# q in 512-byte pieces for two chunks at once, some transposes by DMA, and one searched order for the whole kernel: a linear-attention and expert kernel

## The chip, the cores and the metric

The kernel runs on one core of a Trainium2 chip. The metric is the device time of one execution in microseconds (us), median of several runs. A profiled run also gives a trace; its "span", from the first to the last instruction, is about 1.7 us shorter than the time (156.4 against 158.06 us before the change). All runs compared here are of the state "fast" unless a sentence says otherwise. "TensorE" does the matrix products and (PE in the profile) also transposes; VectorE is DVE, ScalarE is ACT, GpSimd is POOL, and SPq is the one queue from which all DMAs of this kernel are issued. PSUM is the memory into which this kernel's TensorE operations write; VectorE or ScalarE copies a result out of it ("evacuates" it) before its tile is written again.

## The reference

q, k and v have the shape (4, 8, 768, 64): batch, heads, tokens, head size. A decaying state is summed over the tokens, and its product with q is the input of a feed-forward block.

```python
def _attn_ref(q, k, v):                       # gamma differs by head, scale = 1/8
    for t in range(S):
        state = gamma * state + einsum('bhd,bhe->bhde', k[:, :, t], v[:, :, t])
        y[:, :, t] = scale * einsum('bhd,bhde->bhe', q[:, :, t], state)
def _moe_ref(x, w_in, w_out, g_ln):           # x: 3072 x 512
    h = x @ w_in                              # "first product", 512 -> 1024
    solu = h * softmax(h)
    ln = (solu - mean(solu)) / sqrt(var(solu) + 1e-6) * g_ln
    return ln @ w_out                         # "second product", 1024 -> 512
```

## The kernel before

The tokens are cut into 24 chunks of 128 (six per batch). A chunk needs its 128 x 512 slices of q, k and v as float32 (256 KB each). They are cast to bfloat16; q and k are transposed on TensorE through the one PSUM tile `Tp` (4 blocks of 128 x 128 each) and copied out. `scores` (k times q), `mask`, `intra` (masked scores times v) and `inter` (state times q) give y; then follow the first product `mm1`, `e = exp(h)`, `u = h * e`, eight transposes of u through the same `Tp`, and the second product `mm2`.

```python
def load(name, t, src, slot):                 # one chunk, 256-byte pieces (64 floats)
    op("sp", lambda e: e.dma_start(out=dst[:], in_=src[b, :, rows, :].rearrange("h p d -> p h d")), ...)

def t_in(t, j):                               # 4 transposes of k (j=1) or q (j=0)
    for blk in range(4):
        op("pe", lambda e, blk=blk: e.transpose(
            out=Tp[:, 4 * j + blk, :], in_=qk16[s16][:, j, 128 * blk:128 * blk + 128], identity=ident[:]), ...)

def t_u(t, eng, hf):                          # 8 transposes of u in two halves, then u_evac copies Tp to uT
    for blk in range(4 * hf, 4 * hf + 4):
        op("pe", lambda e, blk=blk: e.transpose(out=Tp[:, blk, :], in_=u16[s][:, ...], identity=ident[:]), ...)
# ... cut: scores, mask, intra, inter, state, mm1, expo, umul, square, stats, mm2, z_out, store
```

Every helper adds its instruction to one program list. A wait is derived from what the instruction reads and writes, and each engine runs its instructions in the order of that list. So the order of the list is the schedule. It comes from three places: a table for the start (`PROLOGUE`), a regular loop for the middle chunks, and a table for the end (`EPILOGUE`). An entry such as `uT.3:act` is a stage, a chunk and, where it isn't the default one, an engine. `warm.5` is five matmuls on constants that only keep TensorE busy while data are on their way.

The softmax here doesn't subtract the row's maximum and nothing guards it: scores larger than these inputs give would overflow.

Of the kernel before, what the change touches and what calls it, by code (L numbers as in the profile page):

```python
# [6 lines left out]
ACT = mybir.ActivationFunctionType  # L7
# [6 lines left out]
L = 128  # L14
# [11 lines left out]
PROLOGUE = """  # L26
Lg.0 warm.6 clr.0 t_g.0 Lk.0 ck.0:dve t_k.0 g_out.0:act Lq.0 Lq.1 cq.0:dve warm.2 t_q.0 qkT.0 Lk.1 cq.1 warm.5
scores.0 Lv.0 Lwi.1 Lwi.0 wi0.0 Lwi.3 ck.1:dve t_k.1 t_q.1 mask.0 wi1.1 Lwi.2 qkT.1:dve cv.0 warm.4 state.0
intra.0 Lv.1 wi1.0 scores.1 Lk.2 mask.1 y.0 Lq.2 Lv.2 wi0.1:dve wi0.2:dve st.0 Lk.3 Lwo.1 wi1.3 wi0.3 Lq.3 Lwo.0
wi1.2 warm.17 mm1_0.0 e0.0 cv.1 ck.2:dve Lwo.2 inter.1 mm1_1.0 state.1 e1.0 intra.1 cq.2 u0.0 y.1 t_k.2 Lwo.3  # L30
warm.2 t_q.2 Lv.3 st.1:act mm1_0.1 qkT.2:dve inter.2 u1.0 e0.1 Lk.4 scores.2 Lq.4 mask.2 Lq.5 cv.2 state.2
mm1_1.1 e1.1 Lv.4 wg.2 sq.0 ck.3 t_k.3 wg.3:dve u0.1 wg.0 cq.3 intra.2 warm.4 t_q.3 y.2 qkT.3:dve warm.3
scores.3 Lk.5 t_u0.0 t_u1.0 st.2 wg.1:dve wg.5 inter.3 u1.1 mm1_0.2 wg.4 wg.6:dve Lk.6 cv.3 mm1_1.2 wg.7 Lv.5
mask.3 uT.0 ck.4 Lq.6 Lv.6 e0.2 u0.2 colmean.0 intra.3 t_k.4 cq.4:dve cm_out.0 statsA.1 sq.1 t_q.4 qkT.4 ctr.3
statsA.0 mm2.0 y.3 cq.5 ctr.0 ctr.1 e1.2 stats.1 ck.5 t_u0.1 cv.4 t_u1.1 Lk.7 zm.0 Lq.7 uT.1:act scores.4
state.3 st.3:act u1.2 mm1_0.3 mask.4 ctr.7 t_k.5 t_q.5 ctr.4 statsA.2 stats.0 e0.3 inter.4 mm1_1.3 state.4 ck.6
cq.6 intra.4 qkT.5 scores.5 st.4:act u0.3 t_u0.2 t_u1.2 mm2.1 e1.3 u1.3 uT.2:act z.0 t_k.6 y.4 t_q.6 zm.1 clr.6
sq.2 cv.6 inter.5 mm1_0.4 Lv.7 statsA.3 qkT.6 store.0 Lk.8 state.6 Lq.8 mm1_1.4 ctr.6 Lv.8 sq.3 ctr.2 z.1
stats.2 t_u0.3 t_u1.3 ctr.5 mm2.2 mask.5 scores.6 e0.4 z.2 cq.7 uT.3 store.1 u0.4 cv.5 Lk.9 intra.5 ck.7 Lq.9
stats.3 Lv.9 e1.4 t_k.7 cv.7 t_q.7 y.5 qkT.7 mm2.3 store.2 Lk.10 ck.8 u1.4 sq.4 Lq.10 Lv.10 t_u0.4 mask.6 st.6  # L40
t_u1.4 uT.4 z.3 mm1_0.5 store.3 mm1_1.5 state.7 e0.5 Lk.11 Lq.11 intra.6 e1.5 Lv.11 ck.9 scores.7 u0.5 u1.5 y.6
cq.8 statsA.4 t_k.8 mask.7 t_q.8 qkT.8 mm2.4 stats.4 t_u0.5 z.4:dve cq.9 t_u1.5 sq.5 mm1_0.6 inter.7 intra.7
scores.8 st.7 uT.5 cv.9 statsA.5 store.4 Lk.12 y.7 mm1_1.6 Lq.12 Lv.12 t_k.9 e0.6 e1.6 u0.6 stats.5 u1.6 t_q.9
qkT.9 mm2.5 ck.10 mm1_0.7 e0.7 t_u0.6 t_u1.6 cv.8 cq.10 inter.8 mm1_1.7 cv.10 z.5:dve store.5 Lk.13 statsA.6
Lq.13 Lv.13 state.8 mask.8 intra.8 sq.6 uT.6 scores.9 t_k.10 t_q.10 stats.6 mm2.6 u0.7 e1.7 u1.7 statsA.7 qkT.10
y.8 z.6:dve t_u0.7 t_u1.7 st.8:act mm1_0.8 mm1_1.8 ck.11 cq.11 cv.11 mask.9 store.6 inter.9 uT.7 Lk.14 Lq.14
sq.7 Lv.14 intra.9 e0.8 state.9 u0.8 scores.10 e1.8 t_k.11 stats.7 u1.8 t_q.11 qkT.11 mm2.7 t_u0.8 sq.8 ck.12
cq.12 cv.12 y.9 st.9 mask.10 t_u1.8 uT.8 z.7 store.7 mm1_0.9 e0.9 mm1_1.9 e1.9 inter.10 Lk.15 Lq.15 statsA.8
Lv.15 intra.10 state.10 scores.11 t_k.12 t_q.12 qkT.12 ck.13 cq.13 cv.13 u0.9 u1.9 y.10 st.10 stats.8 statsA.9
sq.9 stats.9 mm2.8 z.8:dve mask.11 store.8  # L50
"""

EPILOGUE = """
cq.20 Lv.20 intra.15 state.15 scores.16 t_k.17 t_q.17 qkT.17 ck.18 cq.18 cv.18 u0.14 u1.14 y.15 st.15 statsA.14
sq.14 stats.14 mask.16 mm2.13 z.13 store.13 t_u0.14 t_u1.14 uT.14 mm1_0.15 e0.15 mm1_1.15 e1.15 inter.16 Lk.21
Lq.21 Lv.21 intra.16 state.16 cv.20 scores.17 t_k.18 t_q.18 qkT.18 ck.19 cq.19 cv.19 u0.15 u1.15 y.16 st.16
statsA.15 sq.15 stats.15 mask.17 mm2.14 z.14 ck.20 store.14 t_u0.15 t_u1.15 uT.15 mm1_0.16 e0.16 mm1_1.16 e1.16
inter.17 Lk.22 Lq.22 Lv.22 intra.17 scores.18 t_k.19 cq.22 t_q.19 qkT.19 u0.16 u1.16 y.17 statsA.16 sq.16
stats.16 mask.18 mm2.15 z.15 store.15 t_u0.16 t_u1.16 uT.16 mm1_0.17 e0.17 mm1_1.17 e1.17 Lk.23 t_k.20 t_q.20
Lq.23 Lv.23 intra.18 clr.18 state.18 scores.19 u0.17 u1.17 ck.21 cq.21 y.18 ck.22 st.18 qkT.20 statsA.17 sq.17  # L60
stats.17 mask.19 cv.21 mm2.16 z.16 store.16 t_u0.17 t_u1.17 uT.17 mm1_0.18 e0.18 mm1_1.18 t_k.21 t_q.21 e1.18
inter.19 intra.19 state.19 qkT.21 u0.18 u1.18 scores.20 y.19 st.19 mask.20 statsA.18 sq.18 stats.18 mm2.17 z.17
store.17 t_u0.18 cv.22 t_u1.18 inter.20 uT.18 mm1_0.19 e0.19 ck.23:dve intra.20 state.20 y.20 scores.21 mm1_1.19
st.20:act t_k.22 e1.19 u0.19 t_q.22 qkT.22 u1.19 statsA.19 inter.21 sq.19 stats.19 mm2.18 z.18 store.18 cq.23
t_u0.19 t_u1.19 mask.21 mm1_0.20 e0.20 cv.23 intra.21 state.21 uT.19 y.21 scores.22 t_k.23 u0.20 mm1_1.20 t_q.23
st.21:act inter.22 mm1_0.21 mm2.19 mask.22 e1.20 qkT.23 t_u0.20 intra.22 e0.21 u1.20 u0.21 sq.20 mm1_1.21 e1.21
t_u1.20 state.22 y.22 scores.23 uT.20 mm1_0.22 t_u0.21 st.22:act u1.21 z.19 statsA.20 e0.22 statsA.21 inter.23
store.19 sq.21 mask.23 t_u1.21 uT.21 stats.20 mm1_1.22 intra.23 e1.22 u0.22 y.23 mm2.20 stats.21 t_u0.22
mm1_0.23 u1.22 t_u1.22 mm1_1.23 e0.23 statsA.22 z.20:dve uT.22 mm2.21 store.20 e1.23 u0.23 u1.23 z.21:dve
store.21 t_u0.23 t_u1.23 sq.22 sq.23 mm2.22 statsA.23 stats.22 z.22 uT.23 store.22 mm2_0.23 stats.23 z_0.23:dve  # L70
mm2_1.23 z_1.23:dve store_0.23 store_1.23
# [109 lines left out]
def bass_retnet_recurrent__then__act_solu_kernel(  # L181
# [16 lines left out]
    NRAW, N16, NQT, NOUT = 8, 4, 4, 4  # L198
    NUNC = 2
    LAG = 2  # L200

    with ExitStack() as es:
        sb = lambda name, shape, dt: es.enter_context(nc.sbuf_tensor(name, shape, dt))

        q_raw = [sb(f"q_raw{i}", [128, H, D], F32) for i in range(NRAW)]
        k_raw = [sb(f"k_raw{i}", [128, H, D], F32) for i in range(NRAW)]
        v_raw = [sb(f"v_raw{i}", [128, H, D], F32) for i in range(NRAW)]
        qk16 = [sb(f"qk16_{i}", [128, 2, DM], BF16) for i in range(N16)]
        v16 = [sb(f"v16_{i}", [128, H, D], BF16) for i in range(N16)]
        qkT = [sb(f"qkT{i}", [128, 8, 128], BF16) for i in range(NQT)]  # L210
# [53 lines left out]
        def load(name, t, src, slot):  # L264
            dst = {"q": q_raw, "k": k_raw, "v": v_raw}[name][slot]
            b, c = tiles[t]
            rows = slice(c * L, (c + 1) * L)
            op("sp", lambda e: e.dma_start(out=dst[:], in_=src[b, :, rows, :].rearrange("h p d -> p h d")),  # L268
               w=[(name + "raw", slot)], sem=f"ld{name}{slot}")

        def load_k(t, eng):
            load("k", t, k, t % NRAW)

        def load_q(t, eng):
            load("q", t, q, t % NRAW)

        def load_v(t, eng):
            load("v", t, v, t % NRAW)

        def load_w_in(kt, eng):  # L280
            op("sp", lambda e: e.dma_start(out=w_in_st[:, kt, :], in_=moe_w_in[128 * kt:128 * kt + 128, :]),  # L281
               w=[("w_in_st", kt)], sem=f"w_in{kt}")
# [19 lines left out]
        def setup_consts():  # L302
            op("dve", lambda e: e.memset(ones_bf[:], 1.0), w=["ones_bf"])
            op("pool", lambda e: e.iota(iota_c[:], [[128, NCH]], base=1, channel_multiplier=1,
# [4 lines left out]
            op("pool", lambda e: e.affine_select(out=tri[:], in_=ones_bf[:], pattern=[[1, 128]],  # L309
# [6 lines left out]
            op("pool", lambda e: e.iota(iota_t[:], [[1, S]], base=1, channel_multiplier=0,  # L316
# [11 lines left out]
            op("dve", lambda e: e.memset(zeros_bf[:], 0.0), w=["zeros_bf"])  # L328
# [14 lines left out]
        def w_in_cast(kt, eng, hf):  # L343
            cols = slice(512 * hf, 512 * hf + 512)
            copy_scaled(eng, w_in16[:, kt, cols], w_in_st[:, kt, cols], SCALE,
                        r=[("w_in_st", kt)], w=[("w_in16", kt, hf)])
# [27 lines left out]
        def cast(name, j, raw, t, eng):  # L374
            s, s16 = t % NRAW, t % N16
            src, dst = raw[s][:].rearrange("p h d -> p (h d)"), qk16[s16][:, j, :]
            f = (lambda e: e.activation(out=dst, in_=src, func=ACT.Copy)) if eng == "act" else (
                lambda e: e.tensor_copy(out=dst, in_=src))
            op(eng, f, r=[(name + "raw", s)], w=[(name + "16", s16)])

        def cast_k(t, eng):
            cast("k", 1, k_raw, t, eng)

        def cast_q(t, eng):
            cast("q", 0, q_raw, t, eng)
# [9 lines left out]
        def evac(eng, out, in_, **deps):  # L395
            if eng == "act":
                op(eng, lambda e: e.activation(out=out, in_=in_, func=ACT.Copy), **deps)  # L397
            else:
                op(eng, lambda e: e.tensor_copy(out=out, in_=in_), **deps)  # L399

        def t_in(t, j):
            s16 = t % N16
            for blk in range(4):
                op("pe", lambda e, blk=blk: e.transpose(  # L404
# [313 lines left out]
```

## Time and profile before

| | before |
|---|---|
| time, median | 158.06 us (157.45 to 158.09) |
| span of the profiled run | 156.4 us |
| busy: TensorE, VectorE, ScalarE, GpSimd | 94%, 76%, 68%, 59% of the span |
| share of the DMA queue over 16 engines | 80.7% |
| TensorE transposes, warm-up matmuls | 384, 43 |

Busy time by stretch, kernel before. The columns are the stretch, its length, busy us and instruction count of TensorE, of its weight loads, of VectorE, ScalarE and GpSimd, the granted TensorE clock, the busy share of the DMA engines and the rate that they moved.

```profile
core 0: us, PE busy (x) PEld busy (x) DVE busy (x) ACT busy (x) POOL busy (x), PEclk, DMA share, GB/s
0.00:16.00 16.00, 12.33 (x86) 5.71 (x87) 8.63 (x31) 9.36 (x14) 3.48 (x12) 1.00 0.99 251
16.00:33.00 17.00, 14.43 (x142) 7.44 (x141) 12.20 (x24) 9.78 (x21) 6.46 (x11) 1.00 1.09 258
33.00:70.00 37.00, 36.46 (x390) 21.15 (x388) 32.08 (x59) 27.56 (x54) 31.98 (x61) 1.00 1.09 239
70.00:96.00 26.00, 26.00 (x259) 15.10 (x256) 21.10 (x39) 18.79 (x37) 18.39 (x40) 1.00 0.88 194
96.00:117.00 21.00, 21.00 (x230) 12.78 (x228) 16.99 (x31) 15.36 (x30) 14.04 (x29) 1.00 0.90 197
117.00:154.00 37.00, 36.69 (x361) 21.39 (x359) 28.19 (x53) 25.43 (x54) 18.42 (x47) 1.00 0.26 77
```

From 33 us on TensorE is busy for practically all of each stretch: it is the limit there. Before 33 us the DMA share is about 1 at some 255 GB/s, and 43 of TensorE's matmuls there are warm-ups: the loads are the limit. The chain of waits, cut to one chunk in the middle (start, us on the chain, what):

```profile
80.44 0.55 PE Tp L404 x8
80.99 1.73 PE Zp L550 x8
82.72 0.45 PE Tp L531 x8
83.17 1.73 PE Hp L480 x8
```

The chain stays on TensorE. It shows what an operation costs where TensorE is the limit: eight transposes 0.45 us (56 ns each), a full product 1.73 us. Five to six us pass between one first product and the next. The page's lines on packets and on the DMA queue:

```profile
DMA packets 80178, 29.61 MB, mean 189 GB/s; under 512 B 75416, under 2 KB 75680, under 8 KB 80160
...
q1 hardware_dynamic: 80160, 29.37, 80.7%
```

75,416 of the 80,178 packets are under 512 bytes, nearly all of them q, k and v (72 x 1,024 pieces of 256 bytes). The start of the first product, from the timeline of TensorE (start, us, what, count):

```profile
14.67 1.24 PE L369 MATMUL Zp<-ones_bf,zeros_bf 128*128 128x512 bf16 x5
15.75 1.03 PE L480 MATMUL Hp<-w_in,xT 128*128 128x512 bf16 x4
```

### The profile page before, as it was taken

Reading aid. Unit: us, or ns where it says so; the run is one execution under the profiler, and the core shown is the slowest. Engines: PE = TensorE matmul, PEld = TensorE weight load, DVE = VectorE, ACT = ScalarE, POOL = GpSimd, SP = SyncE. Lnnn points to the kernel's source line nnn. Section 1 sums busy time; section 2 is a strip of 40 time slices with the busy share of each in tenths; the row PEclk is TensorE's granted clock in tenths of the full one; section 3 lists DMA queues with packets and bytes.
Section 4 is the critical chain, followed back from the end, with each engine's and each line's share of the span. In section 5 each row is a group of like instructions: output and inputs, shape, how many; then the busy total and the mean of one; then the engine's idle time right before and its main releaser. Section 6 shows DMA issues by size and latency. Waiting matters only on the chain.

```text
span 156.4 us, 3798 instructions
## 1 busy us (share of the span) xinstructions
PE 146.9 (94%) x1456; PEld 83.6 (53%) x1456; DVE 119.4 (76%) x234; ACT 106.3 (68%) x210; POOL 92.8 (59%) x195
## 2 busy tenths in 40 slices
PE   0999989689998999999999999999999999999993
PEld 0454544245645556565655566566555656555552
DVE  6257588689997796798796877796878698859752
ACT  6628436948978645868667776876877768669370
POOL 4120441389999897699486578409978661705260
PEclk9999999999999999999999999999999999999999
DMA  4999999998998999999986996996897610101113
GB/s 94 228 368 316 201 254 357 232 225 183 241 257 201 262 267 223 266 263 196 222 200 163 178 229 152 201 228 165 191 191 185 150 66 9 67 4 67 67 67 134
DMA packets 80178, 29.61 MB, mean 189 GB/s; under 512 B 75416, under 2 KB 75680, under 8 KB 80160
## 3 DMA queue, kind: packets, MB, share of 16 engines
q1 hardware_dynamic: 80160, 29.37, 80.7%
q8 instruction: 11, 0.18, 0.5%
q14 instruction: 7, 0.06, 0.1%
HBM read 23.07 MB, written 6.29 MB: 188 GB/s over the span
## 4 chain that ended last, share of the span: by engine, by line
PE 68%; SPq 15%; POOL 6%; DMA 4%; DVE 4%; issue 1%; DVEq 0%
PE Zp L550 22%; PE Hp L480 21%; SPq L268 11%; PE Tp L404 6%; PE Tp L531 6%; DMA q_raw<-in_q_dram 4%; PE Yp L448 4%; PE PT L422 4%; SPq L285 3%; PE Yp L438 2%; PE PT L550 2%; SPq L281 2%; PE Sp L464 1%; DVE w L362 1%; POOL chain L512 1%
## 5 line engine op out<-in xcount | busy, mean ns | idle before, releaser
L480 PE MATMUL Hp<-w_in,xT 128*128 128x512 bf16 x192 | 47.3, 379 | 0.0
L550 PE MATMUL Zp<-w,uT 128*128 128x512 bf16 (+1 forms) x168 | 38.9, 374 | 0.0
L429 DVE TENSOR_TENSOR ptm<-PT,tri 128x1024 bf16<-128x1024 f32 x24 | 29.2, 1216 | 1.9 <-PE PT L422 1.9
L397 ACT ACTIVATE qkT<-Tp 128x1024 bf16<-128x1024 bf16 x21 | 21.4, 1020 | 12.4 <-PE Tp L404 12.4
L480 PEld LDWEIGHTS Hp<-w_in,xT 128*128 128x128 bf16 x192 | 17.0, 98 | 15.5 <-DVE su L493 0.4
L550 PEld LDWEIGHTS Zp<-w,uT 128*128 128x128 bf16 x168 | 15.6, 98 | 15.2
L487 ACT ACTIVATE e_1<-Hp 128x512 bf16<-128x512 f32 x24 | 14.3, 596 | 13.6 <-PE Hp L480 13.6
L487 ACT ACTIVATE e_0<-Hp 128x512 bf16<-128x512 f32 x24 | 14.3, 595 | 9.6 <-PE Hp L480 9.6
L474 DVE TENSOR_TENSOR xT<-Yp,ytab 128x512 bf16<-128x512 f32 x24 | 16.4, 685 | 2.3 <-PE Yp L448 2.2
L399 DVE COPY uT<-Tp 128x1024 bf16<-128x1024 bf16 x22 | 15.0, 683 | 1.8 <-PE Tp L531 1.5
L369 PE MATMUL Zp<-ones_bf,zeros_bf 128*128 128x512 bf16 x43 | 12.1, 419 | 3.6 <-DVE zeros_bf L328 3.6
L519 POOL TENSOR_SCALAR chain<-sq,chain 128x1 f32<-128x1 f32 x24 | 7.4, 308 | 12.9 <-ACT sq_junk L502 11.9
L525 POOL TENSOR_TENSOR rstd<-chain,mhalf 128x1 f32<-128x1 f32 x24 | 13.2, 549 | 2.0
L502 ACT ACTIVATE sq_junk<-u_1 128x1024 bf16<-128x1024 bf16 x12 | 12.6, 1051 | 0.1
L502 ACT ACTIVATE sq_junk<-u_0 128x1024 bf16<-128x1024 bf16 x12 | 12.6, 1049 | 0.0
L509 POOL TENSOR_SCALAR chain<-se 128x1 f32<-128x1 f32 x24 | 6.7, 280 | 9.9 <-ACT e_1 L487 8.4
L493 DVE CUSTOM_DVE_ANT_0 u_1<-Hp,e_1 128x512 bf16<-128x512 f32 x12 | 8.2, 686 | 5.6 <-ACT e_1 L487 5.6
L493 DVE CUSTOM_DVE_ANT_0 u_1<-Hp,e_1,su 128x512 bf16<-128x512 f32 x12 | 9.0, 750 | 3.5 <-ACT e_1 L487 3.5
L339 ACT ACTIVATE out_sb<-Zp,rstd 128x512 f32<-128x512 f32 x14 | 9.5, 679 | 2.4 <-PE Zp L550 2.4
L493 DVE CUSTOM_DVE_ANT_0 u_0<-Hp,e_0 128x512 bf16<-128x512 f32 x12 | 8.2, 683 | 3.0 <-ACT e_0 L487 3.0
L493 DVE CUSTOM_DVE_ANT_0 u_0<-Hp,e_0,su 128x512 bf16<-128x512 f32 x12 | 9.0, 748 | 1.9 <-ACT e_0 L487 1.8
L512 POOL TENSOR_SCALAR chain<-su 128x1 f32<-128x1 f32 x24 | 7.4, 309 | 4.7 <-DVE su L493 3.2
(106 smaller groups left out, 261.3 us busy)
## 6 DMA issues: line engine op xcount, KB each, us to landing
k_raw<-in_k_dram SPq DMA_DIRECT2D x24, 256.0 KB, 4.1
q_raw<-in_q_dram SPq DMA_DIRECT2D x24, 256.0 KB, 4.4
v_raw<-in_v_dram SPq DMA_DIRECT2D x24, 256.0 KB, 4.7
out_dram<-out_sb SPq DMA_DIRECT2D x23, 256.0 KB, 2.3
w_in_st<-in_moe_w_in_dram SPq DMA_DIRECT2D x4, 512.0 KB, 5.8
w_out_st<-in_moe_w_out_dram SPq DMA_DIRECT2D x4, 512.0 KB, 6.6
out_dram<-out_sb SPq DMA_DIRECT2D x2, 128.0 KB, 1.7
g_row<-in_moe_g_ln_dram SPq DMA_DIRECT2D x1, 4.0 KB
```

Source lines behind the costliest of these rows:

```text
L268: op("sp", lambda e: e.dma_start(out=dst[:], in_=src[b, :, rows, :].rearrange("h p d -> p h d")), w=[(name + "raw", slot)], sem=f"ld{name} ...
L369: op("pe", lambda e: e.matmul(Zp[:], zeros_bf[:], ones_bf[:].unsqueeze(1).to_broadcast([128, 4, 128]), start=True, stop=True), r=["zeros_b ...
L397: op(eng, lambda e: e.activation(out=out, in_=in_, func=ACT.Copy), **deps)
L399: op(eng, lambda e: e.tensor_copy(out=out, in_=in_), **deps)
L429: op("dve", lambda e: e.tensor_tensor(out=ptm[s][:], in0=PT[:], in1=tri[:].unsqueeze(1).to_broadcast([128, 8, 128]), op=ALU.mult), r=["tri ...
L474: op("dve", lambda e: e.tensor_tensor(out=xT[s][:], in0=Yp[:], in1=ytab[:, c, :, :], op=ALU.mult), r=[("ytab", p) for p in range(NPAIR)], ...
L480: op("pe", lambda e, kt=kt: e.matmul(Hp[:, hf, :], xT[s][:, kt, :], w_in16[:, kt, 512 * hf:512 * hf + 512], start=(kt == 0), stop=(kt == K ...
L487: op("act", lambda e: e.activation(out=e16[s][:, 512 * hf:512 * hf + 512], in_=Hp[:, hf, :], func=ACT.Exp, accum_out=se[ss][:, hf:hf + 1]) ...
L493: op("dve", lambda e: e.tensor_tensor_reduce(out=u16[s][:, 512 * hf:512 * hf + 512], in0=Hp[:, hf, :], in1=e16[s][:, 512 * hf:512 * hf + 512],
L502: op("act", lambda e: e.activation(out=sq_junk[:], in_=u16[s][:], func=ACT.Square, accum_out=sq[ss][:]), r=[("u16", s, 0), ("u16", s, 1)], ...
L525: op("pool", lambda e: e.tensor_tensor(out=rstd[ss][:], in0=ch[:, 3:4], in1=mhalf[:], op=ALU.pow), r=[("ch3", sc), "mhalf"], w=[("rstd", ss)])
L550: op("pe", lambda e, kt=kt: e.matmul(dst, uT[s][:, kt, :], w[:, kt, cols], start=(kt == 0), stop=(kt == KT2 - 1)), r=[("uT", s), (wname, k ...
```

## The change

The intent is to take work from TensorE and to make room in the DMA queue for it. Parts:

- q is loaded for a pair of chunks, so that a partition holds two neighbouring tokens, in pieces of 512 bytes. The mask, the decay table, q's columns and the write of xT are adapted to the order of tokens that follows.
- 13 of 24 transposes of u, 5 of k, and 1 of a pair of q become DMA transposes; the rest stay on TensorE.
- w_in comes in column halves, so that the first half of the first product needs 1 MB instead of 2. Three of four matmuls that clear the state become a start flag.
- One table, made by search, gives the order of everything.

```diff
-PROLOGUE = """ ... """     EPILOGUE = """ ... """     # and the loop for the middle
+ORDER = """
+Lq.0 warm.6 clr.0 Lg.0 warm.5 t_g.0 g_out.0:act cq.0:dve t_q.0 Lk.0 Lk.1 ck.0 qT.0:dve Lv.0 warm.3 t_k.0
+... (cut)
-        q_raw = [sb(f"q_raw{i}", [128, H, D], F32) for i in range(NRAW)]
+        q_raw = [sb(f"q_raw{i}", [128, H, 2, D], F32) for i in range(NQRAW)]
+        def load_q(sc, eng):
+            op("sp", lambda e: e.dma_start(out=q_raw[slot][:],
+                in_=q[b, :, c * L:(c + 2) * L, :].rearrange("h (p j) d -> p h j d", j=2)), ...)
+        def d_k(t, eng):
+            op("sp", lambda e: e.dma_start_transpose(out=kT[t % NKT][:], in_=k16[t % N16][:]), ...)
+        def d_q(sc, eng): ...
+        def d_u(t, eng):
+            op("sp", lambda e: e.dma_start_transpose(out=uT[t % 3][:], in_=u16[t % 2][:]), ...)
+        def q_cols(t, rows, p):
+            return qT[t // 2 % NQT][rows, :, p, 64 * (t % 2):64 * (t % 2) + 64]
-                        start=False, stop=True, skip_group_check=True),            # state
+                        start=(t > 0 and tiles[t][1] == 0 and p == 0), stop=True, skip_group_check=True),
# ... cut: w_in in column halves, tri and iota_t by even and odd tokens, xT written with a step of 2
```

## The prediction

> **What bounds the kernel now.** Two stages. (1) From about 33 us to 153.7 us of the 156.4 us span TensorE is the limit: by the view of busy time in stretches it is busy 36.5 of 37 us (33 to 70), 26.0 of 26 (70 to 96), 21.0 of 21 and 36.7 of 37 us. The chain of waits after 47.9 us is all TensorE; a chunk takes 5.3 to 5.7 us there. (2) Before 33 us the loads are the limit: the DMA share is 0.99 to 1.09 at 251 to 258 GB/s, the chain is DMA issues[...], TensorE fills time with 43 warm-up matmuls. Real TensorE work, summed from the chain, is about 5.5 us x 24 + 1.8 us (column mean) = 133.5 us, so about 23 us are lost: 20 at the start, 2.7 in the tail after the last matmul.
>
> **What the change does.** (a) 13 u, 5 k and 1 double-chunk q transposes go to DMA: 13x8 + 5x4 + 1x8 = 132 of the 384 TensorE transposes. Eight cost 0.45 us in the chain, 56 ns each: 7.4 us less, nearly all in stage 1, on the critical path. Their PSUM evacuations go too. (b) Three of four state-clearing matmuls go (0.32 us each in the chain): 1.0 us less. (c) q comes in 512-byte pieces. At DMA share 1.05 the core moves 238 GB/s; [...] (d) w_in comes in column halves, so the first half of the first product needs 1 MB, not 2; this product, now at 15.75 us, should start about 3 us earlier. Warm-ups fall from 43 to 33 (0.22 us each): the start should shrink by 2 to 3 us.
>
> **What it adds.** 13x256 + 1x256 + 5x128 KB = 4.2 MB through DMA transposes. No transpose is in this trace; [...] Most come after chunk 10, where the DMA share falls to 0.26 (117 to 154 us). They share one in-order queue with loads and stores; a late one stalls the second product. VectorE and ScalarE stay at about 118 and 110 us of work in a shorter span, so hand-offs are tighter.
>
> **Predicted time.** 158.06 - 7.4 - 1.0 - 2.5 + 1.4 (waits for transposes and tighter hand-offs) = 148.5 us; range 144.5 to 154.0. Faster by over 2%: 0.87; within 2%: 0.09; slower: 0.04.
>
> **What would show each step.** TensorE transposes 252 instead of 384, TensorE busy about 135 to 139 us, one double product per 4.9 to 5.2 us in chunks 14 to 22; first product starting at 12 to 13.5 us; packets near 68,000 before those of the transposes; waits of the second product for a DMA into uT under 2 us in all; clock still 1.00.
>
> **What would make it wrong.** DMA transposes[...] (under 100 GB/s they take over 40 us of all engines and delay k, v loads), or long issue times on the queue; the strided q columns or xT write being slow; the start not shrinking because k and v still come in 256-byte pieces.

The estimates of queue time, for q's longer pieces and for the transposes, rested on no trace. The trace shows issues of q that took 0.47 to 3.28 us each. The author took the two estimates to balance, so neither is a term of the sum: it keeps all its terms, 158.06 - 7.4 - 1.0 - 2.5 + 1.4 = 148.56, given as 148.5 us.

## The result, and the profile after

The changed kernel takes 150.11 us (149.05 to 150.33, 4 runs) against 158.07 us (157.45 to 159.04, 4 runs). The ratio is 0.9478, with a 95% interval of 0.9411 to 0.9544: faster. A repetition gave 150.55 us and 0.951 (0.9469 to 0.9551). A ratio here is the mean time of one kernel's fast runs over that of the other's of the same rounds, so it is not quite the ratio of the medians quoted.

Busy time by stretch, changed kernel, with the columns of before:

```profile
0.00:16.00 16.00, 13.59 (x103) 5.81 (x103) 9.56 (x33) 9.48 (x16) 5.16 (x13) 1.00 0.98 257
16.00:33.00 17.00, 13.36 (x126) 6.94 (x126) 14.04 (x29) 11.43 (x24) 8.01 (x13) 1.00 1.13 278
33.00:70.00 37.00, 34.79 (x397) 20.39 (x396) 32.71 (x57) 28.16 (x57) 29.08 (x50) 1.00 1.26 223
70.00:96.00 26.00, 26.00 (x279) 14.74 (x277) 21.70 (x40) 19.67 (x46) 20.70 (x40) 1.00 1.16 230
96.00:117.00 21.00, 21.00 (x199) 10.98 (x196) 16.85 (x31) 14.24 (x33) 13.34 (x30) 1.00 0.97 228
117.00:148.00 31.00, 28.79 (x217) 14.65 (x216) 21.63 (x42) 16.45 (x38) 16.67 (x43) 1.00 0.84 195
```

The span fell from 156.4 to 148.5 us and TensorE's busy time from 146.9 to 137.5. TensorE is still busy without a gap from 70 to 117 us. Two things differ from before: between 33 and 70 us it now idles 2.2 us (37.00 less 34.79) where it idled 0.5, and the DMA share is 0.84 in the last stretch, where it was 0.26. The chain of waits of the changed kernel, one late chunk:

```profile
101.19 1.73 PE Zp L581 x8
102.92 0.25 PE Sp L493 x8
103.17 0.23 PE Yp L477 x8
103.39 0.33 PE PT L455 x8
103.72 0.97 PE Hp L511 x4
104.69 0.45 PE Tp L426 x8
105.14 0.86 PE Hp L511 x4
```

The line of eight u transposes is missing here; only q's remains. In chunks 14 to 22 a first product starts every 4.85 us on average (from 93.8 us for chunk 14 to 132.6 us for chunk 22). The page's lines on packets and queue:

```profile
DMA packets 85713, 33.92 MB, mean 228 GB/s; under 512 B 68152, under 2 KB 80704, under 8 KB 85696
...
q1 hardware_dynamic: 85696, 33.70, 105.7%
```

The share is the sum of the times that packets took, as a part of 16 engines' span; at 105.7% some of these times overlap. The start of the first product, timeline of TensorE:

```profile
11.59 0.38 PE L467 MATMUL Yp<-qT,st_1 128*128 128x128 bf16 x4 [0.21 <-ACT st_1 L410]
12.40 1.04 PE L511 MATMUL Hp<-w_in,xT 128*128 128x512 bf16 x4 [0.42 <-ACT w_in L352]
```

The DMA issues of the changed kernel (what, queue, count, size where shown, median us from issue to landing), cut:

```profile
k_raw<-in_k_dram SPq DMA_DIRECT2D x24, 256.0 KB, 5.2
...
uT<-u_1 SPq DMA_TRANSPOSE x8, 3.5
uT<-u_0 SPq DMA_TRANSPOSE x5, 4.3
kT<-k_3 SPq DMA_TRANSPOSE x3, 5.2
```

The one queue issues them one after another: in its timeline a load of k at 41.48 us (1.10 us), a transpose of u at 42.70 us (3.09 us), the next loads of k from 45.83 us.

And the two longest waits of TensorE after its start (who, for whom, us in total, times, longest):

```profile
PE Sp L493 <- POOL v_2 L403: 2.4, 2, 1.3
...
PE Tp L426 <- POOL q_0 L389: 1.0, 1, 1.0
```

No wait of TensorE for a DMA transpose is in that view. What it does wait for are casts of q and v on GpSimd, whose own waits lead back to loads (the longest of these lines: 3.8 us in all for v, 2.3 us for q). Asked for 70 to 148 us alone, the view of TensorE's waits lists none, as it does for the kernel before.

### The profile page after: what moved, and what is told of

It is laid out like the page before. It is cut to its first block, busy times and chain, and to the rows that moved or that the text cites. A ratio compares the mean times of both kernels' runs of the same rounds, so it can differ in the third digit from the quotient of the medians.

```text
span 148.5 us, 3513 instructions
## 1 busy us (share of the span) xinstructions
PE 137.5 (93%) x1311; PEld 73.5 (49%) x1311; DVE 116.5 (78%) x227; ACT 99.4 (67%) x208; POOL 93.0 (63%) x185
## 2 busy tenths in 40 slices
DMA packets 85713, 33.92 MB, mean 228 GB/s; under 512 B 68152, under 2 KB 80704, under 8 KB 85696
## 3 DMA queue, kind: packets, MB, share of 16 engines
q1 hardware_dynamic: 85696, 33.70, 105.7%
## 4 chain that ended last, share of the span: by engine, by line
PE 61%; SPq 19%; POOL 9%; DMA 8%; issue 1%; DVE 0%; POOLq 0%
PE Zp L581 22%; PE Hp L511 21%; SPq L271 12%; DMA q_raw<-in_q_dram 4%; DMA k_raw<-in_k_dram 4%; PE PT L455 3%; PE Yp L477 3%; PE Sp L493 2%; SPq L298 2%; PE Tp L426 2%; PE Tp L562 2%; SPq L292 2%; PE Yp L467 2%; PE PT L581 2%; PE Tp L416 2%
## 5 line engine op out<-in xcount | busy, mean ns | idle before, releaser
L511 PE MATMUL Hp<-w_in,xT 128*128 128x512 bf16 x192 | 48.1, 380 | 0.7 <-ACT w_in L352 0.4
L503 DVE TENSOR_TENSOR xT<-Yp,ytab 128x512 bf16<-128x512 f32 x24 | 17.7, 736 | 9.2 <-PE Yp L477 7.4
L556 POOL TENSOR_TENSOR rstd<-chain,mhalf 128x1 f32<-128x1 f32 x24 | 13.5, 564 | 2.0
L382 PE MATMUL Zp<-ones_bf,zeros_bf 128*128 128x512 bf16 x33 | 10.6, 446 | 1.2 <-DVE ones L326 1.2
L410 ACT ACTIVATE kT<-Tp 128x512 bf16<-128x512 bf16 x11 | 6.6, 596 | 6.0 <-PE Tp L416 5.9
L354 DVE TENSOR_SCALAR out_sb<-Zp,rstd 128x512 f32<-128x512 f32 (+1 forms) x12 | 8.7, 726 | 2.2 <-PE Zp L581 1.7
L543 POOL TENSOR_SCALAR chain<-su 128x1 f32<-128x1 f32 x24 | 6.8, 282 | 5.7 <-DVE su L524 4.2
L553 POOL TENSOR_SCALAR chain<-chain 128x1 f32<-128x1 f32 x24 | 8.6, 357 | 2.6
L524 DVE CUSTOM_DVE_ANT_0 u_1<-Hp,e_1 128x512 bf16<-128x512 f32 x12 | 8.2, 684 | 2.1 <-ACT e_1 L518 1.9
L455 PE MATMUL PT<-qT,kT 64*128 64x128 bf16 x192 | 9.5, 219 | 0.1
L389 POOL CAST k_2<-k_raw 128x512 bf16<-128x512 f32 x6 | 4.1, 690 | 7.5 <-DMA k_raw<-in_k_dram 7.4
```

What stands on the lines that cost most here:

```text
L354: op(eng, lambda e: e.tensor_scalar(out=out, in0=in_, scalar1=scale, scalar2=None, op0=ALU.mult), **deps)
L382: op("pe", lambda e: e.matmul(Zp[:], zeros_bf[:], ones_bf[:].unsqueeze(1).to_broadcast([128, 4, 128]), start=True, stop=True), r=["zeros_b ...
L455: op("pe", lambda e, p=p, h2=h2, rows=rows: e.matmul(PT[:, 4 * h2 + p, :], kT[t % NKT][rows, p, :], q_cols(t, rows, p), start=True, stop=T ...
L503: op("dve", lambda e: e.tensor_tensor(out=xT[s][:].rearrange("q k (p j) -> q k j p", j=2), in0=Yp[:].rearrange("q k (j p) -> q k j p", j=2 ...
L511: op("pe", lambda e, kt=kt: e.matmul(Hp[:, hf, :], xT[s][:, kt, :], w_in16[:, kt, 512 * hf:512 * hf + 512], start=(kt == 0), stop=(kt == K ...
L524: op("dve", lambda e: e.tensor_tensor_reduce(out=u16[s][:, 512 * hf:512 * hf + 512], in0=Hp[:, hf, :], in1=e16[s][:, 512 * hf:512 * hf + 512],
```

## The experiments

Twelve kernels ran. My theory (A): the gain is TensorE's saved work, on the critical path in full, and the DMA transposes cost little where they were put. Its rivals: the transposes give much back through the queue (B), the longer pieces of q make the gain (H), TensorE has slack after the change (E), and the gain needs the new order (D). Theories F, G and I to L concern single points. An edit by hand in a table made by search is not searched again; several runs below show what that costs.

### e1: the transposes left out

```diff
 # ORDER without its 19 entries du.*, dk.*, dq.*; the readers use what the tile held before
-... Lk.9 du.3 kT.7 ...   -... inter.8 du.5 e1.6 ...   -... (17 more)
```

> The changed kernel with all 19 DMA transposes left out and nothing in their place (results wrong on purpose: the later chunks use old transposed data). TensorE's work and order are those of the changed kernel. Theory A (the transposes cost little where they are): 148.5 to 150 us, at most 1.5 us under the changed kernel's 150.1. Rival B (their DMA time and their place in the one queue give back a large part of the 7.4 us that they save on TensorE): 145 to 147 us. The DMA share of the queue tells what the 4.2 MB cost[...].

Measured: 149.17 us (148.74 to 149.71), ratio 0.9459 (0.9395 to 0.9523). That is 0.9 us under the changed kernel's 150.11 and 1.4 us under its 150.55, which were taken in other rounds; by the ratios, each to the kernel before in the same rounds, it is 0.3 and 0.8 us, and the intervals overlap. So with TensorE's work and order unchanged, the DMA transposes themselves cost about 1 us or less: theory A holds for the time. The queue is another matter. Page lines of e1:

```profile
DMA packets 68209, 29.59 MB, mean 201 GB/s; under 512 B 50648, under 2 KB 63200, under 8 KB 68192
...
q1 hardware_dynamic: 68192, 29.37, 79.7%
```

The queue's time is 0.797 x 147.1 = 117.2 us of all engines, against 1.057 x 148.5 = 157.0 in the changed kernel. The 4.3 MB of transposes (4,224 KB, the prediction's 4.2) account for 39.8 us. They make 85,713 - 68,209 = 17,504 packets, about 250 bytes each. The small cost in time and the 39.8 us of queue time fit together by where the packets run. The last two stretches of e1, to set beside those of the changed kernel (some matmul records are missing from this trace, so only the DMA share, 0.46 and 0.23, is read here):

```profile
96.00:117.00 21.00, 20.68 (x217) 11.28 (x219) 16.06 (x30) 13.99 (x32) 12.72 (x30) 1.00 0.46 122
117.00:148.00 31.00, 27.23 (x184) 13.75 (x186) 20.90 (x42) 15.33 (x37) 14.45 (x38) 1.00 0.23 86
```

With the transposes the shares are 0.97 and 0.84. That is 21 x 0.51 + 31 x 0.61 = 29.6 of the 39.8 us, in a part of the kernel where the queue was otherwise half to three quarters empty.

### e2: all transposes back on TensorE

```diff
-du.19                                # and so for 13 du, 5 dk, 1 dq
+t_u0.19 t_u1.19 uT.19               # at the next place, after some TensorE work, where Tp is free
```

> The changed kernel with all 19 transposes put back on TensorE (132 more transposes, 8 to 4 at a time, with their evacuations), at hand-picked places in the same order. Theory A: 132 x 56 ns = 7.4 us back, less 0 to 1.5 us of relieved DMA, plus some us since the order is not searched again: 156 to 159 us. Rival B: 152 to 154.5 us, since DMA contention falls away.

Measured: 177.02 us, ratio 1.1198 (1.112 to 1.1276), result right. Neither theory named anything like it. In the trace TensorE waits for evacuations of `Tp` again and again (two of its groups of waits are shown), idles 7 of the 43 us from 117 to 160 us, and its granted clock falls to 0.6 in two of the 40 slices of the page.

```profile
PE Tp L562 <- ACT uT L410: 3.5, 3, 1.2
...
PE Tp L416 <- ACT uT L410: 2.0, 2, 1.1
```

The run doesn't price the transposes; its waits point to the 19 more passes through the single `Tp` tile, which, put in by hand, break the order. Run e5 was made to price them without that.

### e3: q in 256-byte pieces again

```diff
-    in_=q[b, :, c * L:(c + 2) * L, :].rearrange("h (p j) d -> p h j d", j=2)     # one DMA
+    in_=q[b, :, (c + j) * L:(c + j + 1) * L, :].rearrange("h p d -> p h d")      # two DMAs, j = 0, 1
-    return qT[t // 2 % NQT][rows, :, p, 64 * (t % 2):64 * (t % 2) + 64]
+    return qT[t // 2 % NQT][rows, t % 2, p, :]
 # tri, iota_t and the write of xT as in the kernel before
```

> The changed kernel with q in 256-byte pieces again (two DMAs for a pair of chunks; mask, decay table, q columns and xT write in plain token order; result right). Theory A (the 512-byte pieces pay for the transposes[...]): 151 to 153 us[...]. Rival C (the DMA queue has slack where it matters, or k and v decide): 149.6 to 150.6 us; the strided xT write, 736 ns after against 685 before, goes back to 685 in any case.

Measured: 155.9 us (153.6 to 156.6), result right; fast runs give 0.9801 (0.969 to 0.9911). Two of four runs were slow, so the fast mean rests on 153.6 and 155.79. By the ratios it is 3.2% of the time before, about 5 us, over the changed kernel: more than theory A, and rival C falls. The queue's time rose by 5.0 us (1.052 x 154.0 = 162.0 us against 157.0); the author's estimate of it is cut from the expectation. The edit also issues twice as many DMAs for q (24 instead of 12); what of the loss is the pieces and what the issues was not separated. The stretches in question of e3, and what TensorE waited for in the first:

```profile
30.00:34.00 4.00, 0.89 (x21) 0.69 (x22) 3.96 (x8) 2.11 (x5) 2.88 (x3) 1.00 1.20 217
34.00:38.00 4.00, 4.00 (x26) 1.67 (x21) 1.98 (x5) 0.84 (x2) 2.02 (x3) 0.57 1.07 205
```

```profile
32.14 0.61 PE L426 MATMUL Tp<-ident,q 128*128 128x128 bf16 x8 [2.09 <-POOL q L389]
33.77 0.32 PE L493 MATMUL Sp<-v,k 128*64 128x64 bf16 x8 [1.02 <-POOL v L403]
```

q of chunks 4 and 5 comes so late, and then a v, that TensorE is busy for only 0.89 of 4 us, and in the next 4 us its granted clock is 0.57. The idling came in two pieces, 2.09 and 1.02 us, with 0.61 us of transposes between them; how long an idle time it takes to lower the clock, this trace does not show.

### e4: u by DMA in the kernel before

```diff
 # kernel before; t in {11, 12, 13, 15, ..., 22}
-u1.t ... t_u0.t t_u1.t uT.t
+u1.t du.t ...
```

> The kernel before, its order kept, with the u transposes of 11 late chunks (11, 12, 13, 15 to 22) moved to DMA. Theory A (TensorE is the limit there, 0.45 us per chunk are saved): 158.1 - 11 x 0.45 = 153.1 us, 152.5 to 154.5. Rival D (the gain needs the searched order; in the old order each transpose comes too late for the second product): 156 us or more, with waits of the second product for a DMA into uT.

Measured: 156.39 us (155.49 to 157.04), ratio 0.9904 (0.9838 to 0.997), result right. The old order keeps 1.5 us of the 4.95 us (11 x 0.45) that TensorE no longer has to do. Rival D's number fits. TensorE's waits for DMAs into uT:

```profile
PE Zp L537 <- DMA uT<-u: 2.3, 4, 1.0
```

These 2.3 us and the 1.5 us gained leave about 1 us of the 4.95 unaccounted for.

### e5: TensorE's saving given back as empty work

```diff
+        def pad(n, dst, bank):               # 8 per u, 4 per k, 8 for q
+            for _ in range(n):
+                op("pe", lambda e: e.matmul(dst, zeros_bf[:], ones_bf[:], start=True, stop=True), ...)
 # before mm2 of the 13 chunks, and before the scores that use the moved k and q
```

> The changed kernel as it is, with its DMA transposes, plus 132 idle matmuls of 128 columns on TensorE (8 before the second product of each chunk whose u goes by DMA, 4 or 8 before the scores of each chunk whose k or q does), so that TensorE's work is as if nothing had been moved to DMA, with no evacuation and no new order. Theory A (TensorE is the limit from some 70 us on): 132 x 56 ns = 7.4 us more, 156.5 to 158 us. Rival E (the changed kernel has slack on TensorE, it is bound by hand-offs): under 154.5 us.

Measured: 157.76 us (157.31 to 158.66), ratio 0.9969 (0.9915 to 1.0024), result right. 7.4 us of empty 128-column matmuls cost 7.7 us (157.76 less 150.11; 7.2 against the repetition). This is the plainest run: TensorE's time is on the critical path almost in full, and 7.4 us of it is nearly all that the change gained. Theory A holds and rival E falls.

The run also answers a rival that had no letter: that a newly searched order is faster by itself, whatever moves to DMA. Here the new order, q's longer pieces, the halves of w_in and the three clearings saved (1.0 us) are all in place, only TensorE's transposes are made good by empty work, and the time is that of the kernel before. The empty matmuls don't pass through `Tp` and need no evacuation, so the answer is not complete.

### e6: e3 with TensorE kept busy at the gap

```diff
-t_q.2 e1.2 cm_out.0
+e1.2 cm_out.0 warm.12 t_q.2          # in the kernel of e3
```

> Run e3_q_256_bytes again with 12 idle matmuls (2.6 us) in the place where TensorE waited 3.1 us for q of chunks 4 and 5 at 31 to 34 us and where its granted clock then fell to 0.57 for 4 us. Theory F (a third to a half of the 5.8 us that 256-byte pieces cost is the lowered clock after that wait): 152.5 to 154 us, clock 1.00 from 34 to 38 us. Rival G (all of it is late data): 155.5 to 156.5 us with the clock at 1.00.

Measured: 154.84 us (154.01 to 156.05), ratio 0.9784 (0.9717 to 0.985). The stretches of e6:

```profile
30.00:34.00 4.00, 2.99 (x16) 1.29 (x15) 3.96 (x8) 1.24 (x5) 2.75 (x3) 1.00 1.10 229
34.00:38.00 4.00, 3.84 (x44) 2.25 (x42) 2.94 (x5) 2.99 (x5) 1.54 (x3) 1.00 1.12 211
```

The clock stays at 1.00, but the time moves from 0.9801 to 0.9784, well inside the intervals. It falls between the two expectations. The lowered clock was real, and its share of e3's loss is small or not resolved. That the rest is late data is argued from TensorE's waits for casts of q, k and v, not measured apart from the doubled number of DMAs.

### e7: q in 512-byte pieces in the kernel before

```diff
-    load("q", t, q, t % NRAW)
+    if t % 2 == 0:                       # one DMA for the pair
+        op("sp", lambda e: e.dma_start(out=q_raw[slot][:],
+            in_=q[b, :, c * L:(c + 2) * L, :].rearrange("h (p j) d -> p h j d", j=2)), ...)
-    src = raw[s][:]
+    src = raw[s // 2][:, :, t % 2, :]    # nothing else adapted: result wrong on purpose
```

> The kernel before, its order kept, with q loaded for two chunks at a time in 512-byte pieces (result wrong on purpose: the rows of a pair are dealt out even and odd and nothing else is adapted; the time is what counts). Theory A (before 33 us the loads are the limit, after it TensorE): 156 to 157.5 us, gain only at the start. Rival H (the pieces are the larger half of the gain, as the 5.8 us of e3_q_256_bytes suggest): 151.5 to 154 us.

Measured: 157.31 us (156.47 to 157.9), ratio 0.993 (0.9877 to 0.9984): 1.1 us, as theory A says. Rival H falls. The queue's line of e7:

```profile
q1 hardware_dynamic: 67680, 29.37, 73.6%
```

0.736 x 156.1 = 114.9 us of all engines against 126.2 before (0.807 x 156.4): the longer pieces, in half as many DMAs, save 11.3 us of queue time. In the old order, where TensorE is the limit from 33 us on and the DMA share falls to 0.88, 0.90 and 0.26 in the stretches after 70 us, little of that is worth time. In the new order, whose queue share is 105.7%, losing it costs about 5 us (e3).

### e8: both in the kernel before

> The kernel before with both: q in 512-byte pieces (result wrong on purpose, as in e7_before_q_512) and the 11 late u transposes by DMA, in the old order. If the two parts add without the search: 158.07 - 1.5 (e4_before_u_by_dma) - gain of e7_before_q_512. Theory I (in the old order the loads and the transposes compete, and the smaller q frees the room that e4 lacked): 151.5 to 153.5 us, more than the sum. Rival D (the transposes come too late in the old order, whatever the loads do): 154.5 to 156 us.

The edit is that of e4 and e7 together. Measured: 155.96 us (155.41 to 156.87), ratio 0.9868 (0.9811 to 0.9924): 2.1 us by the ratio, no more than the sum of e4 and e7. Theory I falls, and rival D's number fits. TensorE's waits for DMA in e8:

```profile
PE Zp L546 <- DMA uT<-u: 2.7, 2, 1.9
```

The longest, 1.9 us, is the second product at 96.8 us. In the old order a second product comes about one chunk after its u is ready, some 5 us.

### e9: more lead in the old order

```diff
 # loop of e8
-for n in ("mm2", "zm", "z", "store"): put(n, j - LAG)
+for n in ("mm2", "zm", "z", "store"): put(n, j - LAG - 1)
 # EPILOGUE: mm2, z and store of chunks 13 to 20 one chunk later
```

> Run e8_before_q_512_u_by_dma (156.0 us) with the second product of chunks 9 to 20 one chunk later in the old order, so that each DMA transpose has about 10 us instead of 5 before its result is needed (result wrong on purpose, as in e8). Theory J (in the old order the transposes were issued too close to their use, and the order made by search gives them the lead): the waits of the second product for a DMA, 2.7 us in e8, vanish and the time falls to 152.5 to 154 us. Rival K (the missing 3 us lie in hand-offs between the engines): 155 us or more.

Measured: 155.82 us (155.77 to 156.34), ratio 0.9848 (0.9802 to 0.9894). The waits for DMA are gone from the view, as theory J says, but the time is that of e8. TensorE's waits of e9, cut:

```profile
PE Tp L396 <- POOL qk L370: 1.6, 3, 0.9
PE Tp L523 <- ACT qkT L389: 1.2, 1, 1.2
PE Zp L546 <- ACT out_sb L327: 0.8, 1, 0.8
```

From 70 us to its last product TensorE's waits are now 3.1 us in all (the view of stretches leaves some 4 us, but 25 matmul records are missing from this trace), at other places: for a cast of q and k on GpSimd, for `Tp`, and for the one PSUM bank of the second product, since the delayed products pile up at the end. So of theory J the waits are right and the time is not, and rival K's number holds (155 us or more): more lead removes the waits for DMA, and other hand-offs, which did not show before, take their place. What an order would do that was searched for exactly this work was not tried.

### e10 and e11: the transposes placed otherwise, and e12: the changed kernel again

```diff
 # e10                                        # e11: e10, and in place
-du.3   +t_u0.3 t_u1.3 uT.3:act               -t_u0.14 t_u1.14 uT.14   +du.14
-du.5   +t_u0.5 t_u1.5 uT.5                   -t_k.t kT.t   +dk.t     # t = 17, 18, 21, 22
```

> The changed kernel with only the two early u transposes (chunks 3 and 5, issued at 43 and 52 us while loads fill the queue) back on TensorE at hand-picked places. Theory L (these two cost the loads about 1.4 us, as the milestones of e1_no_transposes show, and save 0.9 us of TensorE): 149 to 150 us, 0.3 to 1 us under the changed kernel. If the early transposes are harmless: 150.5 to 151.5 us.

> e10_early_on_pe, and in exchange u of chunk 14 and k of chunks 17, 18, 21 and 22 by DMA, issued in place in the same order: 24 transposes less on TensorE, 24 x 56 ns = 1.35 us. If late transposes cost nothing, as e1_no_transposes says: 1.0 to 1.4 us under e10. If the queue is full there (the DMA share from 96 us on is 0.84 to 0.97), late data give it back: equal to e10 or up to 3 us above.

> The changed kernel as it is, on the same chip as e9 to e11, to compare them with: 149.5 to 150.5 us, ratio to the kernel before 0.945 to 0.952.

Measured: e10 152.54 us (151.85 to 153.35), ratio 0.9637 (0.9592 to 0.9682), result right. On the same chip e12 took 150.55 us, ratio 0.951 (0.9469 to 0.9551). Theory L falls. The two transposes that run among the loads (a DMA share of 1.26 from 33 to 70 us in e12) do cost queue time (0.953 x 150.6 = 143.5 us in e10 against 1.052 x 148.7 = 156.4 in e12): 12.9 us for two, 6.5 each, where the eleven late ones of e8 cost 20.7 (135.6 less 114.9 in e7), 1.9 each. Why the early ones take more packet time was not shown. Yet taking them off the queue makes the kernel 2.0 us slower: 0.9 us is TensorE's own work; that the rest comes from `Tp` and from placing by hand is argued, not measured.

e11 spread from 153.08 to 158.3 us. Only its first run is fast; the others are slow, at a granted clock of 0.978 to 0.989. No ratio comes of that, but even the fast run is not under the medians of e10 or e12, so there is no sign that five more late transposes gained anything. Why five of six runs were slow, at a lower clock, is open: no trace of a slow one was kept. In the trace of the fast run one lost place shows. VectorE's waits from 95 to 125 us, cut, and TensorE's timeline (start, us, what, idle before and its releaser):

```profile
DVE u L521 <- DMA uT<-u: 2.8, 1, 2.8
```

```profile
111.20 1.04 PE L508 MATMUL Hp<-w_in,xT 128*128 128x512 bf16 x4 [1.93 <-DVE su L521]
```

u of chunk 14 is read by a DMA transpose that the queue begins to issue at 105.95 us, after two loads of v. VectorE may not overwrite that u buffer (there are two) until the transpose has landed, and waits 2.8 us; TensorE then waits 1.93 us for VectorE. Here the DMA transpose held its source for about 4.4 us from issue (105.95 to some 110.4 us), where eight transposes on TensorE take 0.45 us. No version with a right result beat the changed kernel.

## Why the prediction was right

It named 148.5 us with a range of 144.5 to 154.0, and 150.11 was measured. Point by point:

- **TensorE's work is the limit and the saving counts in full.** Right. Chain and stretches said so, and e5 shows it: 7.4 us of work given back cost 7.7 us.
- **The start shrinks by 2.5 us.** This term was too large. The first product starts at 12.40 us as forecast (12 to 13.5), but by chunk 2 the lead is 1.0 us (25.3 against 26.3 us), since the next loads, not w_in, decide. How far the kernels are at 70 us follows from the end: both are then busy without a gap to their last product, at 145.8 and 153.7 us. Of that difference of 7.9 us, work removed after 70 us makes up 6.9 (eleven u at 0.45, four k at 0.22, one q at 0.45, two clearings at 0.32), which leaves 1.0 us for everything before 70 us, where the work removed (two u, one k, one clearing) alone is 1.4 us. The better start was spent again on the 2.2 us of idling from 33 to 70 us.
- **The transposes' cost on the queue, balanced by q's longer pieces.** Wrong as to the balance; both terms were estimates. q's pieces save 11.3 us (e7), though in the new order losing them cost only 5.0 (e3). The transposes take 39.8 us (e1), 12.9 of it with the two early ones (e10 against e12). That is 109 GB/s, at the edge of what the prediction itself named as making it wrong (under 100 GB/s, over 40 us). It hardly moved the time because 29.6 us of it fell where the queue was not full (a DMA share of 0.46 and 0.23 in e1). The prediction had named that place; that it could hold so much was not known beforehand, and was luck.
- **1.4 us for waits and hand-offs.** Too large for the place it was meant for: the transposes cost 0.3 to 0.8 us by the ratios of e1, none of it is a wait of the second product for a DMA, and after 70 us TensorE has no wait at all in the view. The time fell by 7.95 us where the first two terms, 7.4 and 1.0, make 8.4: start and waits together, forecast as 1.1 us gained, came out as some 0.4 us lost. That is nearly the whole miss of 1.6 us. Both terms were too large, with opposite signs, so the sum came nearer than its parts; that is luck, too.
- **The checks.** 252 transposes (8 x 11 of u, 4 x 19 of k, 8 x 11 of q), TensorE busy 137.5 us (forecast 135 to 139), 68,209 packets without the transposes (forecast 68,000) and a clock of 1.00 came out; the distance of first products, 4.85 us, is just under the forecast 4.9 to 5.2.

One thing the prediction named as a risk but took to be settled by the order: that a late transpose's latency is hidden. In the old order it isn't (e4, e8: 1.5 and 2.1 us gained where 11 u transposes alone are 5.0 us of TensorE). Each part of the change that was tried alone in the old order is worth little. In the searched order 7.4 us of saved work became time (e5), and there the form in which q is loaded is worth about 5 us (e3). Whether another order in the old style could have done the same is not known.

## What to carry to other kernels

Where one engine is busy without a gap, price a change by that engine's work on the chain, and check it by giving the work back as empty instructions (7.4 us given back cost 7.7, e5). Work moved to an idle resource paid in full here only in an order made for it (1.5 of 4.95 us in the old one, e4): look at when its result is needed and at which buffer it holds meanwhile. A saving on a queue that has slack shows little alone (1.1 us in e7), and can still be what a second change lives on (about 5 us in e3).

## What the runs measured of DMA transposes and of the clock

- 4.3 MB of transposes from on-chip memory to on-chip memory took 39.8 us of all engines' packet time, 109 GB/s, among other traffic (e1 against the changed kernel); 2.9 MB took 20.7 us (135.6 in e8 less 114.9 in e7), 139 GB/s. By the same measure all the other traffic moved at 251 GB/s (29.37 MB in 117.2 us, e1). From issue to landing, 3.5 to 5.5 us in the median of a group, they are like loads of k (5.2 us).
- The transposes made 17,504 packets of about 250 bytes for 4.3 MB (e1 against the changed kernel).
- On the issuing queue of the changed kernel a transpose of 128 x 1024 elements took 1.24 us at the shortest, where a plain load of 256 KB took 0.38 us at its shortest.
- The granted clock was 0.57 over 4 us of e3, after waits of 2.09 and 1.02 us with 0.61 us of transposes between; in e6, with TensorE busy for 2.99 us of the 4 us before, it was 1.00. In e2 a second product took 3.48 us instead of 1.89 (at 141.75 us), after 4.1 us with nothing but 24 transposes and 2.3 us of waits. How long an idle time lowers the clock, and what the transposes count for, these runs don't show.
